# One-bank PSUM tiles in the gate, a stage of its own for the Newton steps, and k turned on TensorE

## The chip, the cores and the metric

The kernel runs on one core of one Trainium2 chip. The metric is the time of one execution on the device in microseconds (us); where a kernel ran several times, the median is given. One core has no other die to compare with, so an execution counts as disturbed (slow) when it is more than 1.5% above the fastest of the same kernel. Ratios are the mean time of one kernel's fast runs over the mean of the other's fast runs of the same rounds, so they are not quite the ratio of the medians quoted beside them.

The engines are called as in the profile: PE is TensorE's matrix multiplication, PEld its weight loading, ACT ScalarE, DVE VectorE, POOL GpSimd (which issues the loads), SP SyncE (which issues the transposes and the stores).

## The reference, cut to what matters

```python
# 8 batches, 8 heads, 576 positions, head size 64; m = 32 landmarks
q_lm, k_lm = means of q and of k over blocks of 18 positions
A  = softmax(q @ k_lm.T / 8); Bm = softmax(q_lm @ k_lm.T / 8); C = softmax(q_lm @ k.T / 8)
Z  = Bm.T / (norm1(Bm) * norminf(Bm) + 1e-6)
for _ in range(6): Z = 2 * Z - Z @ Bm @ Z          # Newton steps
x  = A @ Z @ C @ v                                 # heads side by side: 576 x 512
x1, x2, x3 = split(x @ w_proj, 3)                  # 512 -> 3 * 512
conv = irfft(rfft(x2, axis=1) * rfft(filter), n=576)
out  = (x1 * conv * x3) @ w_out
```

## The kernel before

For each batch there are three pieces of work. `front` makes landmarks, Bm and the start of Newton; `back` makes the six Newton steps, the two sets of scores, C v, and the normalised A with its transpose AT; `gate` makes the projection, the Fourier transform by matrix multiplication, the product with the filter, the inverse transform and the two factors x1 and x3. `project` is the output projection of the batch before, put in small steps into the gate. A batch's `back` and the next one's `front` are woven ahead of the gate of the batch before. The framework's scheduler decides the final order of the instructions on each engine.

The eight PSUM banks (512 fp32 columns each) were divided so:

```python
ps_w = tile_pool(name="ps_w", bufs=2, PSUM)   # gate, filter, projection: 2 tiles of 2 banks
ps_f = tile_pool(name="ps_f", bufs=2, PSUM)   # front
ps_k = tile_pool(name="ps_k", bufs=2, PSUM)   # back
def wtile(): return ps_w.tile([P, 2, 512], F32, tag="w", name="w")
```

The gate fills a tile of two banks and one instruction empties both:

```python
def g_part(jb):
    pg = wtile()
    for g in range(2):
        for pp in range(2):
            mm(pg[64*pp:64*pp+64, g, :], ZC[...], wproj[...], start=True, stop=True)
    nc.scalar.copy(G[:, :, Dm*jb:Dm*(jb+1)], pg)             # 1024 columns
...
for part in (0, 2):                                          # the factors x1 and x3
    px = wtile()
    for g in range(2):
        for e in range(2):
            mm(px[:, e, 0:HS], G[...], AT[:, g, HS*e:HS*e+HS], start=(g==0), stop=(g==1))
    if part == 0: x1 = ...; nc.scalar.copy(x1, px[:, :, 0:HS])   # 576 columns
    else: nc.vector.tensor_tensor(gt[:, ji], px[:, :, 0:HS], x1, op=ALU.mult)
```

Both q and k, which lie with positions on the partitions, are turned by DMA, one transpose after the other on one queue, for each batch:

```python
nc.sync.dma_start_transpose(kT, kn)     # in front(b)
nc.sync.dma_start_transpose(qT, qn)
```

The softmax here doesn't subtract the row's maximum and nothing guards it: scores larger than these inputs give would overflow.

## Time and profile before

| of the kernel before | |
|---|---|
| time, median of 3 runs | 278.95 us (275.12 to 279.15) |
| span of the profiled run | 277.0 us |
| PE, DVE, ACT, POOL busy | 81, 66, 57, 15% |
| y (the gated product) of batch 1, 5, 6, 7 ends at | 115.44, 219.11, 244.81, 266.84 us |

The end of y is a good milestone: it is the last thing a gate makes, and the gates follow each other strictly. The prediction below shows the page, the stretches and the last gate. Three rows of the page's groups show what the wide tiles cost. A row gives line, engine, operation, what is made from what, shapes and count; then busy us and mean ns of one; then the idle us of that engine just before them and what ended most of it.

```profile
L541 PE MATMUL w<-AT,G 128*128 128x288 f16 x256 | 40.3, 285 | 6.1 <-ACT G L472 3.0
L548 DVE TENSOR_TENSOR gt<-w,x 128x576 bf16<-128x576 f32 x32 | 24.1, 756 | 15.4 <-PE w L541 7.2
L472 ACT CAST G<-w 128x1024 bf16<-128x1024 f32 x24 | 23.6, 1015 | 5.9 <-PE w L468 5.7
```

The factor matmuls wait 6.1 us, 3.0 of them for G and 2.4 for the emptying of gt's tile, and gt on DVE waits for those matmuls in turn.

### The profile page before, as it was taken

The numbers are of one execution on the slowest core, as the hardware profiler recorded it, in microseconds if no ns is written. First come the engines' busy times: TensorE is split into PE (matmuls) and PEld (weight loads), VectorE is DVE, ScalarE is ACT, GpSimd is POOL, SyncE is SP. The second block draws the span as 40 slices with busy tenths as digits, with TensorE's granted clock in tenths as the row PEclk, the third lists the DMA queues.
The fourth block names the chain that finished last, engine by engine and source line by source line (L and its number), as shares of the span: only waits on it lengthen the run. The fifth ranks groups of instructions, "written<-read, shape, count | busy, mean of one in ns | idle before, by whom it ended". The sixth has DMA issues, their size and how long they took to land.

```text
span 277.0 us, 5760 instructions
## 1 busy us (share of the span) xinstructions
PE 224.3 (81%) x2300; PEld 147.0 (53%) x2300; DVE 183.4 (66%) x429; ACT 158.1 (57%) x269; POOL 40.7 (15%) x91
## 2 busy tenths in 40 slices
PE   0315199798989999999999999899978996896870
PEld 0204065465767557756766676587546743543530
DVE  1492215648878795896799679957985596537531
ACT  1156043259658577839855885598467746465430
POOL 8961220141050410211210001000000000000000
PEclk9999999999999999999999999999999999999998
DMA  6999999999999999999999976900140023005006
GB/s 83 189 150 215 205 197 187 152 211 161 183 153 165 169 130 184 216 177 181 219 179 81 225 156 94 231 22 2 37 116 20 4 76 95 2 25 147 2 0 170
DMA packets 70283, 36.10 MB, mean 130 GB/s; under 512 B 51632, under 2 KB 65456, under 8 KB 70256
## 3 DMA queue, kind: packets, MB, share of 16 engines
q0 software_dynamic: 26480, 16.85, 47.2%
q1 hardware_dynamic: 43776, 18.88, 39.1%
q8 instruction: 18, 0.29, 0.5%
q14 instruction: 9, 0.07, 0.1%
HBM read 33.69 MB, written 9.44 MB: 156 GB/s over the span
## 4 chain that ended last, share of the span: by engine, by line
PE 56%; ACT 13%; DVE 13%; DMA 7%; POOL 4%; issue 4%; DVEq 0%; SPq 0%; POOLq 0%
PE w L589 9%; PE w L541 7%; DMA filt<-in_moe_filter_fft_dram 7%; PE w L478 5%; PE pc L327 5%; PE w L556 4%; DVE gt L548 4%; PE w L468 4%; PE pv L351 4%; PE w L498 3%; ACT G L472 3%; ACT EO L560 2%; PE w L433 2%; PE w L558 2%; ACT X L501 2%
## 5 line engine op out<-in xcount | busy, mean ns | idle before, releaser
L541 PE MATMUL w<-AT,G 128*128 128x288 f16 x256 | 40.3, 285 | 6.1 <-ACT G L472 3.0
L548 DVE TENSOR_TENSOR gt<-w,x 128x576 bf16<-128x576 f32 x32 | 24.1, 756 | 15.4 <-PE w L541 7.2
L589 PE MATMUL w<-wout,y 128*128 128x512 bf16 x128 | 31.9, 378 | 1.6 <-DVE y L565 1.1
L541 PEld LDWEIGHTS <-G 128*128 128x128 bf16 x256 | 23.2, 97 | 17.7 <-ACT G L472 6.4
L560 ACT CAST EO<-w 128x576 bf16<-128x576 f32 x32 | 20.4, 638 | 14.0 <-PE w L558 13.7
L472 ACT CAST G<-w 128x1024 bf16<-128x1024 f32 x24 | 23.6, 1015 | 5.9 <-PE w L468 5.7
L556 PE MATMUL w<-IV,Y 128*128 128x288 f16 x128 | 24.7, 285 | 1.6 <-DVE gt L548 1.5
L546 ACT CAST x<-w 128x576 bf16<-128x576 f32 x32 | 20.6, 645 | 7.3 <-PE w L541 6.4
L501 ACT CAST X<-w 128x1024 bf16<-128x1024 f32 x16 | 16.2, 1014 | 14.7 <-PE w L498 14.7
L318 ACT CAST RZ<-pn 128x256 f16<-128x256 f32 x40 | 15.2, 380 | 13.5 <-PE pn L314 10.0
L503 DVE TENSOR_TENSOR T<-X,HH 128x2048 bf16<-128x2048 bf16 x16 | 19.4, 1215 | 4.4 <-ACT X L501 4.2
L319 DVE TENSOR_TENSOR RZ<-RZ,pn 128x64 f16<-128x64 f16 x48 | 10.3, 215 | 15.6 <-ACT RZ L318 12.0
L314 PE MATMUL pn<-RZ 128*128 128x160 f16 (+1 forms) x96 | 15.3, 236 | 5.7 <-DVE RZ L298 3.3
L81 POOL DMA_DIRECT2D qn<-in_q_dram x16 | 12.4, 782 | 43.1 <-PE ptA L394 16.0
L468 PE MATMUL w<-wproj,ZC 128*64 128x512 bf16 x96 | 16.6, 398 | 2.4 <-ACT X L519 2.1
L478 PE MATMUL w<-F,AE 96*128 96x304 f16 x96 | 18.2, 306 | 0.4 <-ACT G L472 0.2
L558 PE MATMUL w<-IV,Y 128*128 128x288 f16 x64 | 18.3, 286 | 0.0
L589 PEld LDWEIGHTS <-y 128*128 128x128 bf16 x128 | 11.6, 97 | 12.4 <-DVE y L565 1.6
L498 PE MATMUL w<-G,Ah 128*128 128x512 bf16 x64 | 17.0, 378 | 0.0
L563 DVE TENSOR_TENSOR sd<-EO 128x576 bf16<-128x576 bf16 x16 | 7.3, 458 | 14.6 <-ACT EO L560 14.6
L351 PE MATMUL pv<-vb,eC 96*128 96x320 bf16 x96 | 16.7, 320 | 0.1
L376 DVE TENSOR_REDUCE rA<-eA 96x48 f32<-96x1536 bf16 x8 | 13.9, 1743 | 3.7 <-ACT eA L330 3.7
(139 smaller groups left out, 450.6 us busy)
## 6 DMA issues: line engine op xcount, KB each, us to landing
kn<-in_k_dram POOLq DMA_DIRECT2D x8, 576.0 KB, 14.4
qn<-in_q_dram POOLq DMA_DIRECT2D x16, 288.0 KB, 10.4
vb<-in_v_dram POOLq DMA_DIRECT2D x16, 288.0 KB, 12.0
out_dram<-os SPq DMA_DIRECT2D x24, 192.0 KB, 2.7
out_dram<-os SPq DMA_DIRECT2D x16, 128.0 KB, 2.9
wproj<-in_moe_w_proj_dram POOLq DMA_DIRECT2D x1, 1536.0 KB, 16.8
out_dram<-os SPq DMA_DIRECT2D x24, 64.0 KB, 2.6
out_dram<-o SPq DMA_DIRECT2D x16, 64.0 KB, 2.1
```

The lines of the kernel that those rows point to most:

```text
L351: mm(pv[:, 0:320], eC[:, c, 128 * g:128 * g + 128], vn[:, g, :, c, :], start=(c == 0), stop=(c == NC - 1))
L468: mm(pg[64 * pp:64 * pp + 64, g, :], ZC[:, 2 * g + pp, :, :].rearrange("p h l -> p (h l)"), wproj[:, 2 * g + pp, Dm * jb:Dm * (jb + 1)], s ...
L472: nc.scalar.copy(G[:, :, Dm * jb:Dm * (jb + 1)], pg)
L478: mm(pf[:, par, 0:TW], AE[:, par, c, 128 * g:128 * g + 128], F[:, c, par, :], start=(c == 0), stop=(c == 2))
L498: mm(px[:, t, :], Ah[:, g, par, 128 * t:128 * t + 128], G[:, g, Dm:2 * Dm], start=(g == 0), stop=(g == 1))
L501: nc.scalar.copy(X, px)
L541: mm(px[:, e, 0:HS], G[:, g, lo:lo + P], AT[:, g, HS * e:HS * e + HS], start=(g == 0), stop=(g == 1))
L548: nc.vector.tensor_tensor(gt[:, ji], px[:, :, 0:HS], x1, op=ALU.mult)
L556: mm(pi[:, ji, 0:HS], Y[:, par, t, P * j:P * j + P], IV[:, par, t, :], start=(t == 0), stop=False)
L558: mm(pi[:, ji, 0:HS], Y2[:, P * ji:P * ji + P], IV2[:, jp, par, :], start=False, stop=True)
L560: nc.scalar.copy(EO[:, par], pi[:, :, 0:HS])
L589: mm(po[:, u, :], yv[:, j, P * (2 * ip + u):P * (2 * ip + u + 1)], wout[:, j, :], start=(j == 0), stop=(j == 3))
```

## The change

The intent: (1) the four banks of `ps_w` become four tiles of one bank, and all evacuations of the gate become halves; (2) Newton becomes a stage `inverse` between `front` and `back`, with a PSUM bank of its own (taken from `front`), so four batches are in flight; (3) k is turned by 24 transposes of 96 columns on PE, woven between the Newton steps, instead of by DMA; (4) all output copies `os` go to ACT, where VectorE had half of them. The core of the diff:

```diff
-    ps_w = tile_pool(name="ps_w", bufs=2)          -    ps_f = tile_pool(name="ps_f", bufs=2)
+    ps_w = tile_pool(name="ps_w", bufs=4)          +    ps_f = tile_pool(name="ps_f", bufs=1)
+    ps_i = tile_pool(name="ps_i", bufs=1)
     def wtile():
-        return ps_w.tile([P, 2, 512], F32, tag="w", name="w")
+        return ps_w.tile([P, 512], F32, tag="w", name="w")
 ...
-        nc.sync.dma_start_transpose(kT, kn)        # q's transpose moves from front to inverse
+        def turn(i):                               # in inverse(b), after Newton steps 0, 2, 4
+            pt = ktile("pt", BF16)
+            for u in range(8):
+                mm(pt[:, u*R:(u+1)*R], kn[... 8*i+u ...], ident[:R, :R], is_transpose=True, ...)
+            (nc.scalar.copy if i == 1 else nc.vector.tensor_copy)(kT[... chunk i ...], pt[:, 0:8*R])
 ...
         def g_part(jb):
-            pg = wtile()
             for g in range(2):
+                pg = wtile()
                 for pp in range(2): mm(...)
-            nc.scalar.copy(G[:, :, Dm*jb:Dm*(jb+1)], pg)
+                nc.scalar.copy(G[:, g, Dm*jb:Dm*(jb+1)], pg)
 ...  (the same for the forward and inverse transform, X, and the filter)
-    px[:, e, 0:288] of x1 and x3: 4 matmuls of 288 columns, one copy of 576
+    px of x1 and x3: 2 matmuls of 512 columns, one copy of 512;
+    factors_rest(): the last 64 columns of all 8 in one tile, 16 matmuls of 64 columns
 ...
-            (nc.vector.tensor_copy if ip else nc.scalar.copy)(os, po)      # 1024 columns
+            nc.scalar.copy(os, po)                                         # 512 columns
 ...
-        weave(steps(back, b + 1, NK), steps(front, b + 2, NF), ...)
+        weave(steps(back, b + 1, 12), ...)
         gate(b, pending)
+        weave(steps(inverse, b + 2, 10), steps(front, b + 3, 7))
```

## The prediction

> **What bounds the kernel now.** I read the page first (busy shares, slices, chain), then a table of stretches, then the timeline of the last gate, where nothing else runs.
>
> ```profile
> PE 224.3 (81%) x2300; PEld 147.0 (53%) x2300; DVE 183.4 (66%) x429; ACT 158.1 (57%) x269; POOL 40.7 (15%) x91
> ...
> PE   0315199798989999999999999899978996896870
> ...
> DMA  6999999999999999999999976900140023005006
> ```
>
> Each digit is a fortieth of the span, 6.9 us. There are three stages. Up to slice 5 (33 us) PE is nearly idle and the DMA full. From slice 6 to 31 PE shows 7 to 9. In the last eight slices (222 us on) it falls again. The stretches, cut at the recurring output projections, say the same:
>
> ```profile
> core 0: us, PE busy (x) PEld busy (x) DVE busy (x) ACT busy (x) POOL busy (x), PEclk, DMA share, GB/s
> 144.70:170.40 25.70, 25.12 (x277) 17.05 (x275) 20.31 (x49) 18.29 (x32) 1.02 (x2) 1.00 1.02 140
> ...
> 222.00:245.00 23.00, 18.74 (x146) 10.71 (x145) 16.39 (x31) 12.63 (x17) 0.00 (x0) 1.00 0.19 52
> 245.00:277.00 32.00, 20.08 (x137) 10.58 (x135) 13.35 (x20) 12.04 (x16) 0.00 (x0) 0.97 0.27 75
> ```
>
> The middle is a steady 25.7 us per batch, PE busy in 25.1 of them. But that counts pipelined ends. The spacing of starts is the real need: a run of n matmuls lasts (n-1) spacings plus one duration, so 8 of the projection in 1.89 us at 378 ns each give 216 ns; the factor matmuls of 288 columns (4 in 0.65 us, 285 ns each) 122 ns; the transposes ptA (12 in 0.68, 215 each) 42 ns. Summing such spacings over one batch of the middle I get 23.1 us: gate 3.9 (factors) + 2.9 (inverse transform) + 1.7 (X) + 1.6 (forward transform) + 1.6 (G) + 0.5, projection 3.9, scores 2.2, pv 1.6, and about 3.2 for front, Newton and transposes. So about 2.6 us of each 25.7 is waiting, part of it the weight loads of narrow tiles. PE bounds the middle; there is little to win there.
>
> The last gate:
>
> ```profile
> 254.80 0.66 PE L541 MATMUL w<-AT,G 128*128 128x288 f16 x4 [0.67 <-ACT G L472]
> 255.71 1.19 PE L541 MATMUL w<-AT,G 128*128 128x288 f16 x8 [0.25 <-ACT G L472]
> 256.49 0.76 DVE L548 TENSOR_TENSOR gt<-w,x 128x576 bf16<-128x576 f32 x1 [1.81 <-PE w L541]
> 257.30 0.65 PE L541 MATMUL w<-AT,G 128*128 128x288 f16 x4 [0.40 <-DVE gt L548]
> ...
> 258.06 0.76 DVE L548 TENSOR_TENSOR gt<-w,x 128x576 bf16<-128x576 f32 x1 [0.81 <-PE w L541]
> ```
>
> Here is a ping-pong over two buffers: PE fills one, VectorE or ScalarE empties it, PE may go on. All three engines show idle time in brackets. From y of batch 6 (244.8) to y of batch 7 (266.85) it takes 22.05 us for about 14 us of PE spacings.
>
> **What the Trainium skill says.** (1) "PSUM — Partial Sum Buffer", The four PSUM rules: one matmul output is at most one bank, 512 fp32 columns. A wide tile here is two banks, so two tiles are the same four banks as four single ones; the trace agrees in that no matmul exceeds 512 columns. (2) "TensorE: Matmul & The Clock Gate", Back-to-back issue gap: N/2.4 + 2.5 ns when warm, thus 215.8 and 122.5 ns for 512 and 288 columns; the trace has 216 and 122. (3) "VectorE: DVE Perf Modes", The TRN2 errata: ScalarE reading PSUM costs 172 cycles plus one per column at 1.2 GHz[...], so halved tiles pay it twice; that is 997 and 570 ns for 1024 and 512 columns, and the trace has 1015 and 589. (4) "DMA: Bandwidth & Descriptors", Issuing engines are not separate DMA queues: all DMAs share 16 engines. The trace agrees: k transposes take 13.3 us in the median beside loads, but 5.7 us (160.57 to 166.28) where the loads have ended.
>
> **The change part by part.**
>
> *k transposes to PE.* Eight DMA transposes go. 24 PE transposes of 96 columns per batch come: 24 x 42 ns = 1.0 us of PE, in the stage where PE is the bound. Their evacuation is one ScalarE copy of 768 columns, by row G's scaling 640 + 162 = 0.80 us, and two VectorE copies; AT's 576 two-byte columns take 447 ns, so 768 take about 550, 1.1 us together. The relieved DMA matters only before 33 us: the filter lands at 32.7 us and the chain shows 7% of the span for it. The k transpose of batch 0 (7.9 to 13.1 us) mostly precedes the start of that queue's big loads (11.8), so only about 2 us of the 5 come back: -2 us.
>
> *512-column factors.* 32 x 122 = 3.90 us becomes 16 x 215 + 16 x 28 (a 64-column remainder, spaced like pk and pz at 25) = 3.9 us. Nothing for PE.
>
> *Single-bank evacuation.* Consecutive ScalarE copies start a little before the former ends (two G in 1.93 us: 0.91 apart; 512 columns by exp: 0.49). Per batch: G 2.7 to 2.9, Ah 1.1 to 1.2, X 1.8 to 2.0, x1 2.1 to 2.2, EO 2.1 to 2.4, os 0.9 to 2.0 (VectorE's os of 1.2 us moves here), k 0.7. ScalarE goes from 18.1 to about 20.6 us, VectorE stays at 20 (-1.1 os, +0.9 k, +0.1 rest). Both stay below PE.
>
> *Middle, sum.* PE need 23.1 + 1.0 = 24.1. With today's 2.6 us of waiting the batch would be 26.7; finer buffers should take perhaps a third of it, since of some 15 us by which start spacings exceed their usual value between 93 and 196 us (four batches) 4.1 stand before the factors. I choose 26.3: +0.6 over some six batches, +3.5 us.
>
> *Newton as its own stage.* It takes the six-step chain (pn, ScalarE copy, VectorE add) off the way from scores to pv, but in the middle that chain already lies beside the gate; worth nothing there. The last two gates have no Newton left over them, so batch 7's is done earlier.
>
> *Last gate.* From y of 6: PE now has projection 3.44 + X 1.72 + narrow X 0.45 + G 1.1 + rest of projection 0.5 = 7.2 us; with four buffers PE runs ahead of ScalarE (13 copies of 0.49, 6.4 us), so about 7.5 where 9.9 stood (244.9 to 254.8): -2.4. Factors and inverse: PE 6.8, VectorE 5.2 (four gt of 0.61, one of 0.33, four sd, two y), ScalarE 4.6: PE-bound, plus 0.4 in front and 2.4 for the last EO, sd, sd, y behind: 9.6 where 12.05 stood, -2.4. The end: the first output copy ends after 4 instead of 8 matmuls and takes 0.59 instead of 1.01 us, and the ten stores that follow are issued one by one on SP at some 0.5 us each: -0.9. Together -5.7.
>
> *Gates 5 and 6* (196 to 245 us) have the same ping-pong with less work beside them, PE need 21.3 of 26 and 16.7 of 23 us. I give them -1.5 and -2.5.
>
> Sum: -2 + 3.5 - 5.7 - 4 = -8.2 us of 278.95: 270.7, put as **270.5 us**.
>
> **The rivals.** *A: PE pays for it.* The middle is PE-bound and gets 1.0 us more of PE per batch; moreover the front now has one PSUM bank instead of two, so pq must wait until ScalarE has emptied pk (Pk 388 ns plus its queue), and ScalarE stands in line with 2.5 us more work. For it: PE's 9s. Against it: in the built order transposes of k stand between pk and pq as filling. If each batch loses 1.5 us over today, the middle costs +9 and the sum is -3: 276. *B: ScalarE becomes the bound.* 20.6 of some 26 us is 79%, yet in strict order; if os copies wait for PE while X waits behind them, PE stalls in the projection, where 4 os now stand between X copies. That makes 278 to 282. *C: the waits were the true price.* If single banks remove most of the 2.6 us, the batch is 25 us and the kernel 262 to 264. For it: the waits before the factors name G's and gt's evacuation. *D: the DMA was holding the start more than I think* (slices 1 to 20 at 9). Then up to 5 us rather than 2 go there; but PE waits of 34 to 93 us name VectorE's Bn, Cv, A and AT, not loads.
>
> **Range and chances.** A and C are the wide ones, each about a fifth, B a tenth. 80% range 263 to 279. Two per cent is 5.6 us, thus 273.4 and 284.5: faster 0.65, same 0.31, slower 0.04.
>
> **What would show it.** Filter landing near 31 us and first G matmul near 54 (today 56.1); projections in the middle 26.3 us apart with ScalarE busy near 21; k transposes spaced near 42 ns; from y of 6 to y of 7 17 us instead of 22; no DMA transposes of k, and DMA idle digits earlier than slice 25. Wrong would be: a middle period above 27.5 (A or B, told apart by what PE waits for, pk's evacuation or the wide tiles) or below 25.3 (C), or a last gate still above 20 us.

## More of the kernel before

The waits of PE from y of batch 1 to y of batch 5 are small and many (us in total, times, longest):

```profile
PE w L599 <- ACT X L501: 0.7, 1, 0.7
PE w L468 <- ACT X L519: 0.7, 1, 0.7
PE w L541 <- ACT G L472: 0.6, 3, 0.2
PE w L541 <- DVE gt L548: 0.6, 2, 0.4
```

These are four of nine rows. In each a matmul into a w tile waits until ACT or DVE has emptied a w tile; for the third the reason can also be the data, since the factors read the G that this copy makes.

## The result, and the profile after

The changed kernel took 258.39 us (257.89 to 261.96, four runs) where the kernel before took 279.05 us in the same rounds: ratio 0.930, 95% interval 0.917 to 0.942. Its profiled run was the disturbed one, so the same kernel was run again later (five rounds, label after2): 258.21 us against 278.4 us, again 0.930 (0.922 to 0.937). The profile of that second visit is the one read here. The change gained about 20 us, where 8 had been predicted, and the time lies below the predicted range.

From the page of the changed kernel:

```profile
span 256.9 us, 6283 instructions
...
PE 219.9 (86%) x2492; PEld 142.7 (56%) x2492; DVE 185.8 (72%) x446; ACT 188.0 (73%) x401; POOL 40.5 (16%) x91
...
PE   0732099699689999999999999899999999999990
...
DMA  5999999979999996999389944891015002403305
```

From slice 12 on PE shows 8 or 9 up to the last slice but one, where before the last eight slices went down to 6, 6 and 7. ACT did 158.1 us of work before and does 188.0 now: all output copies are its own (18.4 us for 8.1), it has eight copies of k (6.4 us), and halved tiles pay the fixed cost of an evacuation twice (1015 ns for 1024 columns of G before, 604 ns for 512 now). The loads last nearly as long as before (the DMA digits fall at slice 28, 173 us, where they fell at slice 27, 180 us).

The stretches from y to y (us from and to, length, then busy us and count of PE, PEld, DVE, ACT and POOL, granted clock, DMA share, GB/s):

```profile
129.06:155.11 26.05, 25.79 (x305) 16.78 (x303) 21.09 (x52) 21.44 (x49) 3.04 (x5) 1.00 1.01 137
207.80:231.10 23.30, 23.11 (x221) 14.32 (x219) 17.60 (x37) 19.70 (x46) 0.00 (x0) 1.00 0.20 52
231.10:256.90 25.80, 18.83 (x137) 9.50 (x135) 11.16 (x20) 15.07 (x33) 0.00 (x0) 0.93 0.34 92
```

These answer to the three stretches shown in the prediction, cut at y now and not at projections. A batch of the middle takes about the same time as before. The last whole batch (the second row) is shorter and PE is idle in only 0.2 us of it; the last stretch is 25.8 us.

The last gate:

```profile
238.71 1.96 PE L561 MATMUL w<-AT,G 128*128 128x512 f16 x8
...
240.35 1.29 DVE L566 TENSOR_TENSOR gt<-w,x 128x512 bf16<-128x512 f32 x2 [1.63 <-PE w L561]
...
240.51 0.63 PE L575 MATMUL w<-AT,G 128*128 128x64 f16 x16
...
240.98 0.41 PE L588 MATMUL w<-IV,Y 128*128 128x288 f16 x2
...
241.55 1.50 ACT L592 CAST EO<-w 128x288 bf16<-128x288 f32 x4
...
242.45 1.89 PE L561 MATMUL w<-AT,G 128*128 128x512 f16 x8
```

No PE row has brackets: eight factor matmuls run in one stretch while ACT and DVE follow behind. Where before PE stood still after each tile or two, it now runs ahead of its readers. From y of batch 6 to y of batch 7 it takes 16.82 us, where 22.03 us stood.

PE's waits in the middle, from y of batch 1 to y of batch 5, are these two and no more:

```profile
PE pk L218 <- DMA kn<-in_k_dram: 1.0, 1, 1.0
PE pn L325 <- DVE cm L288: 0.2, 1, 0.2
```

The w tiles have gone from the list. Where the 20.1 us between the two profiled spans went, by these milestones:

| stretch | before, us | after, us | difference | predicted |
|---|---|---|---|---|
| start to y of batch 1 | 115.44 | 103.07 | -12.4 | -2 |
| y of 1 to y of 4 | 77.47 | 79.21 | +1.7 | +3.5 over some six batches |
| y of 4 to y of 6 | 51.90 | 48.82 | -3.1 | -4 |
| y of 6 to y of 7 | 22.03 | 16.82 | -5.2 | -4.8 |
| y of 7 to the end | 10.19 | 8.99 | -1.2 | -0.9 |

Everything but the first row is about as predicted. The start gave over ten us more than it was given: -7.8 us up to y of batch 0 (80.56 for 88.31 us), and -4.6 from there to y of batch 1 (22.51 for 27.13 us).

### The profile page after: what moved, and what is told of

Read it like the earlier page. It is cut to its first block, busy times and chain, and to the rows that moved or that the text cites. A ratio compares the mean times of both kernels' runs of the same rounds, so it can differ in the third digit from the quotient of the medians.

```text
span 260.3 us, 6267 instructions
## 1 busy us (share of the span) xinstructions
PE 220.4 (85%) x2476; PEld 143.1 (55%) x2492; DVE 185.3 (71%) x446; ACT 187.9 (72%) x401; POOL 40.8 (16%) x91
## 2 busy tenths in 40 slices
DMA packets 51597, 31.40 MB, mean 121 GB/s; under 512 B 32944, under 2 KB 46768, under 8 KB 51568
## 4 chain that ended last, share of the span: by engine, by line
PE 52%; DMA 22%; issue 11%; POOL 6%; ACT 5%; DVE 3%; POOLq 0%
DMA kn<-in_k_dram 14%; PE w L629 9%; PE w L561 9%; DMA qn<-in_q_dram 7%; PE w L588 4%; PE w L517 4%; PE pv L371 4%; PE pc L351 4%; PE w L486 3%; PE w L496 3%; ACT EO L592 2%; PE w L590 2%; PE pt L314 2%; PE pn L325 1%; PE w L532 1%
## 5 line engine op out<-in xcount | busy, mean ns | idle before, releaser
L561 PE MATMUL w<-AT,G 128*128 128x512 f16 x128 | 32.1, 380 | 0.3
L631 ACT COPY os<-w 128x512 f32<-128x512 f32 x32 | 18.4, 587 | 16.7 <-PE w L629 16.4
L490 ACT CAST G<-w 128x512 bf16<-128x512 f32 x48 | 25.7, 603 | 5.4 <-PE w L486 5.3
L592 ACT CAST EO<-w 128x288 bf16<-128x288 f32 x64 | 24.1, 399 | 1.9 <-PE w L590 1.8
L566 DVE TENSOR_TENSOR gt<-w,x 128x512 bf16<-128x512 f32 x32 | 21.9, 686 | 4.2 <-ACT x L564 2.2
L86 POOL DMA_DIRECT2D qn<-in_q_dram x16 | 12.4, 778 | 73.1 <-PE w L496 17.6
L564 ACT CAST x<-w 128x512 bf16<-128x512 f32 x32 | 19.1, 600 | 5.6 <-PE w L561 4.6
L314 PE MATMUL pt<-ident,kn 96*128 96x96 bf16 x192 | 14.2, 217 | 7.5 <-DMA kn<-in_k_dram 7.5
L519 ACT CAST X<-w 128x512 bf16<-128x512 f32 x32 | 17.8, 593 | 1.2 <-PE w L517 1.2
L486 PE MATMUL w<-wproj,ZC 128*64 128x512 bf16 x96 | 18.6, 401 | 0.0
L561 PEld LDWEIGHTS <-G 128*128 128x128 bf16 x128 | 11.6, 97 | 12.3 <-ACT G L490 2.5
L330 DVE TENSOR_TENSOR RZ<-RZ,pn 128x64 f16<-128x64 f16 x48 | 10.3, 215 | 8.3 <-ACT RZ L329 7.5
```

The source lines that it names most:

```text
L486: mm(pg[64 * pp:64 * pp + 64, :], ZC[:, 2 * g + pp, :, :].rearrange("p h l -> p (h l)"), wproj[:, 2 * g + pp, Dm * jb:Dm * (jb + 1)], star ...
L490: nc.scalar.copy(G[:, g, Dm * jb:Dm * (jb + 1)], pg)
L561: mm(px, G[:, g, lo:lo + P], AT[:, g, 0:512], start=(g == 0), stop=(g == 1))
L566: nc.vector.tensor_tensor(gt[:, j, 0:512], px, x1, op=ALU.mult)
L592: nc.scalar.copy(EO[:, par, j % 2], pi[:, 0:HS])
```

## The experiments

The first theory was that the single-bank tiles made nearly all of the gain, at the start too, and that k on PE is a cost. Its rivals were: that the start is a matter of the clock (the record of the granted clock shows full speed from 60.1 us on in the kernel before, but already from 38.1 us on in the changed one, with a lapse from 48.3 to 51.7, and half-speed matmuls before that); that k's transposes, gone from the DMA, free the start; and that the new stage does it. Where an expectation gives a theory a letter, its own words say what it stands for. All runs gave correct results.

### The parts alone, on the kernel before

**e3_gate**: the kernel before with the changed gate, filter and projection only (four one-bank tiles); k by DMA, no stage of its own for Newton.

```diff
-    ps_w = tile_pool(name="ps_w", bufs=2); wtile: [P, 2, 512]
+    ps_w = tile_pool(name="ps_w", bufs=4); wtile: [P, 512]
+    gate, filter_tables, project as in the changed kernel
```

> The kernel before with only the gate, filter and projection in single-bank tiles. Theory W (waits at the wide tiles were the price in the middle): the middle falls by about 1 to 1.5 us per batch and the last gate from 22 to about 17 us, so 262 to 268 us. Rival S (the own stage for Newton does it): the middle keeps 26 us per batch, only gates 5 to 7 gain, 268 to 273 us.

255.38 us against 277.68 us, ratio 0.921 (0.912 to 0.929). One part alone does more than the whole change. It was run again beside the changed kernel:

> The single-bank gate alone once more, on the same chip as after2: 254 to 256 us if its first result holds, with batches 24.7 us apart.

255.36 us, ratio 0.915 (0.905 to 0.925), where the changed kernel had 258.21 us and 0.930 in the same rounds; the intervals overlap slightly, so the difference of 1% is likely and not certain. In the first profile of it y of batch 1 ends at 106.84 us (-8.6 against before), the four batches of the middle take 99.0 us (-4.7), the next one -3.1, the last gate -5.2, the end -1.2: together -22.8 us. Of the start's 8.6 us, 4.6 lie between y of batch 0 and y of batch 1 (22.55 us, where 27.13 stood). That stretch, first before and then here:

```profile
88.30:115.40 27.10, 26.00 (x293) 17.95 (x292) 21.34 (x52) 19.33 (x35) 3.94 (x6) 1.00 1.36 172
```

```profile
84.30:106.80 22.50, 22.32 (x254) 14.38 (x255) 18.97 (x47) 18.48 (x43) 4.44 (x6) 1.00 1.42 155
```

It is not the same work: PE ran 293 matmuls before and runs 254 now, because fewer scores and Newton steps of later batches fall into it. So the 4.6 us are in part waits that went and in part work that moved to later stretches (from y of 5 to y of 6 it is 197 matmuls, where it was 170). A batch of the middle from the second profile, the same columns as above, and all of PE's waits between 106 and 205 us in it:

```profile
131.08:155.54 24.46, 24.38 (x279) 15.34 (x276) 19.84 (x50) 20.97 (x48) 2.41 (x4) 1.00 1.31 149
```

```profile
PE pc L327 <- ACT eA L330: 0.2, 1, 0.2
```

**e2_kpe**: the kernel before with k turned on PE in `front`, all else as it was.

```diff
-        nc.sync.dma_start_transpose(kT, kn)
+        turn(0); ...; turn(1); ...; turn(2)      # between the parts of front
```

> The kernel before with only k turned on PE (in the front stage, in three parts). Theory C: DMA relief is worth 2 us at the start at most, PE has 1.0 us more per batch; 277 to 285 us unless the clock happens to be granted earlier, which the clock record shows. Theory D: 5 us or more at the start, 270 to 275 us, with the clock still half until about 60 us.

287.77 us, ratio 1.037 (1.028 to 1.046): it costs 10 us. A middle batch takes 27.07 us where 25.92 stood (+1.15), and y of batch 1 comes at 120.43 us, 5 us late. So freeing the DMA of k's transposes is no gain by itself.

**e4_stage**: the kernel before with the stage alone (wide tiles, k by DMA).

```diff
-    ps_f = tile_pool(name="ps_f", bufs=2)
+    ps_f = tile_pool(name="ps_f", bufs=1); ps_i = tile_pool(name="ps_i", bufs=1)
+    def inverse(b): ...                          # Newton, both DMA transposes
```

> The kernel before with the stage of its own for Newton alone (k and q turned by DMA in that stage, front PSUM down to one bank, Newton in its own bank). Theory W: within 2% of the kernel before. Rival S: 268 to 273 us.

269.73 us against 275.67 us, ratio 0.978 (0.968 to 0.988): a gain of some 6 us, though at 2% the verdict is unclear. Its profiled run was a slow one: one middle batch took 29.87 us, the two after it 24.97 and 24.98.

**e8_nostage**: e3_gate and e2_kpe together, no stage.

> The kernel before with single-bank gate and k on PE, Newton left among the scores. If the parts add: 255.4 + 10 = 263 to 267 us. If the stage of its own is what makes room for k on PE, it is above the changed kernel's 258 by 5 us or more; if the stage is worth nothing, 256 to 260 us.

269.1 us, ratio 0.980 (0.973 to 0.987), unclear at 2%. Against e3_gate, k on PE without the stage costs some 14 us (6% by the ratios); a middle batch takes 26.33 us, +1.58 over e3_gate's.

### The parts taken back from the changed kernel

**e6_kdma**: the changed kernel with k turned by DMA again.

```diff
+        nc.sync.dma_start_transpose(kT, kn)      # in inverse, ahead of q's
-                turn(it // 2)
```

> The changed kernel with k turned by DMA again, all else kept. If k on PE costs its 24 spacings of 42 ns per batch, as it did alone in the kernel before (+10 us there): 248 to 253 us. If the DMA relief at the start is worth as much (first G matmul at 46.5 us in the changed kernel against 54.9 with the gate alone): 256 to 261 us.

258.09 us, ratio 0.936 (0.928 to 0.945): the same as the changed kernel. But it comes by the same time in another way. A middle batch takes 24.86 us (1.32 less), and y of batch 0 ends at 89.13 us instead of 80.56. PE's waits between 40 and 90 us begin so:

```profile
PE pc L343 <- DMA qT<-qn: 4.6, 1, 4.6
PE pc L343 <- DMA kT<-kn: 2.0, 1, 2.0
```

With Newton in a stage ahead, the first G matmul comes early (47.3 us, as in the changed kernel), and PE then stands waiting for transposes that queue behind each other. In the changed kernel only q is in that queue: its transposes for batches 1 to 3 end at 52.7, 63.2 and 78.5 us, where here they end at 56.8, 78.7 and 87.3 us. So beside the stage k on PE saves 7 to 9 us at the start and gives them back, 1.3 us in each later batch.

**e7_wide**: the changed kernel with the two wide tiles and the old gate.

> The changed kernel with gate, filter and projection put back into two-bank tiles, stage and k on PE kept. Theory W (the single banks carry the whole gain): it is no faster than the kernel before, 276 to 288 us, and the last gate takes 22 us again. Rival S (the stage carries part of it): 268 to 274 us.

286.04 us, ratio 1.040 (1.033 to 1.047). The single banks are worth 28 us here, but some 13 us of it is an accident of one batch. Of the waits of all engines between 76 and 102 us:

```profile
POOL qn L86 <- DMA qT<-qn: 15.0, 1, 15.0
...
PE pk L218 <- DMA kn<-in_k_dram: 13.1, 1, 13.1
```

A load of q on POOL's queue waited 15 us for the transpose that still read its buffer, the load of k behind it waited too, and PE waited 13.1 us for k. The middle batches beyond it take 26.06 us, against 26.18 in the changed kernel: beside the stage and k on PE, single banks are worth nothing in the middle. They are worth 5.2 us in the last gate (22.04 against 16.82), where Newton and the scores of later batches no longer lie between the tiles. And its y of batch 0, before the accident, ends at 79.30 us, where the kernel before has 88.31 and the changed kernel 80.56. So up to there the changed kernel's gain needs no single banks: the stage and k on PE make it together.

The eight medians together. They come from several calls, whose kernel before had 275.7 to 279.1 us, so differences below 3 us say little:

| us | wide tiles | single banks |
|---|---|---|
| no stage, k by DMA | 277.7 (before) | 255.4 |
| no stage, k on PE | 287.8 | 269.1 |
| stage, k by DMA | 269.7 | 258.1 |
| stage, k on PE | 286.0 (with the accident) | 258.2 (the change) |

The single banks gain in every row. "Single banks" is here the whole changed gate: four tiles, half-size evacuations, factors of 512 columns and output copies on ACT; of these only the output copies were taken back by themselves (g5_osdve). With k by DMA the stage gains beside wide tiles (-8 in the table), not beside single banks (+3). The likely reason is that both remove the same waits. With k on PE it gains beside single banks too (-11). A middle batch with k by DMA takes 25.92 us with neither, 24.75 with single banks, 24.97 with the stage (the batches after the disturbed one), 24.86 with both.

### Is it the clock at the start?

**e1_warm** adds 24 matmuls of 512 columns, whose results nobody reads, to the kernel before, in front of the filter's matmuls, so that the clock is up when these come; landmarks of batch 1 get a lower priority. **e1_ctl** has the change of priority alone.

```diff
+        with tc.high_priority(offset=-400) if b == 1 else nullcontext():   # pk, pq of batch 1
 ...
+            if b == 0 and cc == 2:                                         # e1_warm only
+                pd = wtile()
+                with tc.high_priority(), tc.issue_after(last.ins):
+                    for i in range(24): mm(pd[:, i % 2, :], F[...], F[...], start=True, stop=True)
```

> The kernel before, with 24 matmuls of 512 columns that nobody reads put on PE between the third scores of batch 0 (26 us) and the filter's matmuls (33.7 us), and pk and pq of batch 1 put behind the filter's matmuls. Theory C (clock): in the kernel before PE ran at half its clock until 60 us, and the gain of the changed kernel before its first gate comes from a clock that was granted at 35 us. Then the clock is full by 33 us here, the filter's matmuls start 215 ns apart instead of 426, the first G matmul comes near 49 us instead of 56, and the time is 6 to 9 us below that of the control e1_ctl. Theory D (loads): the gain comes from fewer DMA transposes beside the loads. Then the first G matmul stays within 2 us of 56 and the time within 3 us of the control, since 24 idle-time matmuls change no load.

> The same order of pk and pq of batch 1 as in e1_warm without the 24 matmuls. Both theories: within 1.5% of the kernel before, clock still half until some 50 to 60 us.

277.78 us (0.996, 0.985 to 1.008) and 275.0 us (0.993, 0.986 to 1.001) against 277.68 us. The filter's matmuls, first without and then with the added ones:

```profile
33.71 1.87 PE L436 MATMUL w<-fs,F 96*128 96x512 f16 x4 [7.43 <-DVE fs L427]
```

```profile
35.83 0.81 PE L443 MATMUL w<-fs,F 96*128 96x512 f16 x3
```

The clock did come up: four in 1.87 us, some 426 ns apart, became three in 0.81 us, some 215 ns apart. Yet the first G matmul came at 56.49 us, where the kernel before has 56.05 and the control 52.29, and the time is 2.8 us above the control's, where the clock theory had 6 to 9 us below. The time won was spent in other waits of PE (33 to 57 us of e1_warm):

```profile
PE pq L231 <- DMA qn<-in_q_dram: 4.1, 2, 2.5
PE pk L222 <- DMA kn<-in_k_dram: 2.4, 1, 2.4
```

With these waits the clock fell back to half from 46.4 to 60.0 us, so the test covers the filter's stretch and not all of the start. The control did not do what was expected of it either: its clock was not half until 50 us but full from 37.6 to 47.8 and again from 54.6 us. It has y of batch 1 at 111.65 us, 3.8 us before the kernel before, and from there to the end both take 161.6 us. So an early clock, or the priority alone, goes with 3.8 us at the start; which of the two it is, this pair does not tell.

Two profiles of one kernel are a cleaner test. e3_gate shows full clock only from 57.5 us on, hardly earlier than the kernel before; e3_again, the same kernel, from 41.2 us on with lapses. Their first G matmuls come at 54.87 and 51.57 us, and their y of batch 1 at 106.84 and 105.93 us: the early clock went with 0.9 us. So an early clock is not needed for the gain, and did not bring it where it was forced. But up to some 4 us of the 12.4 at the start may be a matter of the single profile of the kernel before, whose fast runs took 273.5 to 279.6 us in all.

### What of the single banks does it?

The changed gate has smaller evacuations, four tiles instead of two, and a bank that comes back by itself. Two kernels were meant to take these apart, two more ask for other bounds, all from e3_gate and beside a kernel before of 274.18 us.

**g2_bufs2** has half the memory, two one-bank tiles.

```diff
-    ps_w = tile_pool(name="ps_w", bufs=4)
+    ps_w = tile_pool(name="ps_w", bufs=2)
```

> e3_gate with two single-bank buffers instead of four. Theory R: PE can be only one piece ahead, slower than the kernel before, 285 us or more, last gate above 22 us. Rival E: 255 to 265 us.

281.77 us, ratio 1.029 (1.017 to 1.042): slower than before, though at 2% the verdict is unclear. The last gate takes 23.59 us. Theory R's 285 us were not reached; rival E is out.

**g4_pair** has the same four banks and the same half-size evacuations as e3_gate, but hands the banks out as halves of a two-bank tile, which only comes free when both halves are read.

```diff
-        return ps_w.tile([P, 512], F32, tag="w", name="w")
+        if not pair:
+            t = ps_w.tile([P, 2, 512], F32, tag="w", name="w")      # bufs=2
+            pair.extend([t[:, 1], t[:, 0]])
+        return pair.pop()
```

> The gate alone in single-bank pieces (e3_gate), but the pieces come as the two halves of one two-bank tile, so that a half is filled and emptied by itself while PE gets the memory back only when both halves have been read. Theory R (it is the return of buffers one bank at a time): most of the gain goes, 268 to 280 us, last gate above 20 us. Rival E (it is the smaller evacuations, which end sooner and start after half the matmuls): 254 to 260 us, last gate near 17 us.

294.14 us, ratio 1.072 (1.064 to 1.081): nearly 40 us above e3_gate, and outside what either theory gave. A middle batch takes 27.34 us and the last gate 25.91. From the timeline of its last gate, one row of DVE and three of PE:

```profile
269.03 0.69 DVE L551 TENSOR_TENSOR gt<-w,x 128x512 bf16<-128x512 f32 x1 [1.85 <-PE w L546]
269.77 0.59 PE L546 MATMUL w<-AT,G 128*128 128x512 f16 x2 [0.21 <-DVE gt L551]
271.04 0.40 PE L573 MATMUL w<-IV,Y 128*128 128x288 f16 x2 [0.67 <-ACT x L549]
...
271.76 0.63 PE L560 MATMUL w<-AT,G 128*128 128x64 f16 x16 [0.20 <-DVE gt L551]
```

The kernel does not do what its expectation says. The second row fills the second half of the tile whose first half the first row reads, and it begins only when that read is over (269.72 us); the fourth row waits in the same way. Only the third waits for a new tile. A build of this kernel shows it throughout: for all 150 wide tiles the semaphores let PE fill the later half only after the earlier one has been read. So a tile never had more than one half under way, and g4_pair, with four banks, had no more than two pieces under way at a time, like g2_bufs2. It is no test of banks that come back in pairs; that stays untested.

Taken together, the two still answer something. Both have the smaller evacuations and both are slower than the kernel before, so smaller evacuations alone are not it (rival E). Four banks alone are not it either, since g4_pair has them. What e3_gate has and neither of them has is four pieces under way at once, each freed by itself: 255.4 us with four, 281.8 and 294.1 with two.

**g5_osdve** moves every second output copy from ACT to DVE, to see whether ACT bounds e3_gate.

```diff
-            nc.scalar.copy(os, po)
+            (nc.vector.tensor_copy if (i0 // P) % 2 else nc.scalar.copy)(os, po)
```

> e3_gate with two of the four output copies of a batch on VectorE, as in the kernel before. If ScalarE (21 of 24.7 us per batch) stands in the way, 250 to 254 us; if PE bounds the middle, within 1% of e3_gate.

262.17 us, ratio 0.947 (0.935 to 0.959), slower than e3_gate's 0.921 though ACT has less to do (170.4 us of busy time for 176.9); neither expectation came true. DVE has more to do (185.5 for 175.5 us), so the test moves two things at once. It shows that relief of ACT gains nothing here. That ACT does not bound the middle is seen in the row of e3_again above: PE is busy in 24.38 of 24.46 us.

**g7_bufs5** asks whether a fifth tile would gain more: no stage, k by DMA, five one-bank tiles, the fifth taken from `front`, which is left with one.

> e3_gate with five single-bank buffers for the gate and one bank less for the front stage. If waits for gate buffers are still there: 250 to 254 us. If four are enough: within 1% of e3_gate, or slower by the front's lost bank.

260.19 us, ratio 0.939 (0.927 to 0.951; the profiled run was a slow one). A middle batch takes 24.56 us and the last gate 16.80, against 24.75 and 16.81 with four: hardly any use there. The start has y of batch 0 at 90.31 us, where e3_gate has 84.29. That the bank is missed in `front` is likely and not shown, for this slow profile also has half the clock up to 65.9 us.

### A version that takes both

If k on PE pays at the start and costs later, it should be used at the start alone. **h1_first3** is the changed kernel with k on PE in the first three batches and by DMA in the others, **h2_first2** the same with two.

```diff
+        if b >= 3:                                # h2_first2: 2
+            nc.sync.dma_start_transpose(kT, kn)
 ...
-                turn(it // 2)
+                if b < 3:
+                    turn(it // 2)
```

> The changed kernel once more. If stage and k on PE take back more than they give: 1% or more above e3_again (258 against 255). If the difference was one of calls: within 0.5% of it.

> The changed kernel with k turned on PE for batches 0 to 2 and by DMA from batch 3 on, when the loads have less in hand. If k on PE saves at the start and costs 1.15 us per later batch: second y near 103 us, later batches 24.9 instead of 26.0 us apart, so 250 to 253 us. If both effects are not so separate: 256 us or more.

> The same for batches 0 and 1 only: 250 to 254 us if the third batch's transpose no longer meets the rush of loads, 254 to 258 if it does.

Against 278.4 us before and 258.21 us of the changed kernel, h1_first3 takes 251.55 us (0.907, 0.897 to 0.917) and h2_first2 253.17 us (0.911, 0.904 to 0.917). A middle batch of h1_first3:

```profile
127.14:151.98 24.84, 24.80 (x284) 15.70 (x283) 19.87 (x49) 21.14 (x49) 2.66 (x4) 1.00 1.18 179
```

It has the early start of the changed kernel (y of batch 0 at 80.11 us) and the middle of e6_kdma (24.85 us a batch, where the changed kernel has 26.18). It is 2.6% faster than the changed kernel by the medians, and the fastest of all that were run; it is 1.5% below e3_again, where the intervals overlap (0.897 to 0.917 and 0.905 to 0.925). Whether two or three batches are better stays open: the intervals overlap.

## Why the prediction was right or wrong

**Right: the last gate and the end.** -2.4 and -2.4 were given for the last gate and -0.9 for the end; -5.2 and -1.2 were measured. The reading behind it, that four tiles let PE run ahead of its readers, is what the timeline shows; with two such tiles (g2_bufs2) the last gate takes 23.59 us. Gates 5 and 6, given -4 together, gave -3.1.

**Nearly right: the price of k on PE.** 24 x 42 ns = 1.0 us per batch was given; the pairs of kernels with and without it show 1.15, 1.32 and 1.58 us. The trace has eight of these transposes in 0.50 us at 206 ns each, (0.50 - 0.206) / 7 = 42 ns apart, as assumed; the rest is what comes with them.

**Right as a sum, not in its parts: the middle.** 26.3 us a batch were predicted and 26.18 measured. "finer buffers should take perhaps a third of it", about 0.9 of 2.6 us of waiting, was rather low: single banks alone took 1.2 us (25.92 to 24.75). And "worth nothing there", said of the Newton stage, is wrong with wide tiles, where the stage took 0.95 us (25.92 to 24.97, in undisturbed batches of a slow run), and right with single banks, which leave it nothing to take.

**Wrong: the start.** The failed step is "so only about 2 us of the 5 come back: -2 us", which was all that the whole stretch up to y of batch 1 was given. It measured -12.4, and this term alone makes 10.4 of the 12 us by which the time was missed. The step looked at the DMA's loads only. Two things stood in its place.

First, up to y of batch 0 (-7.8 us), the stage and k on PE together, by a path that the prediction did not see. e7_wide, which has these two and wide tiles, has y of batch 0 at 79.30 us, where 88.31 stood. The stage brings the first G matmul from 56.1 to about 47 us (46.00 in e4_stage, 46.59 in e7_wide), and this is only kept when q's transposes no longer queue with k's. With single banks, each of the two without the other loses it: e6_kdma waits 6.6 us for transposes and has y of batch 0 at 89.13 us; e8_nostage has its first G at 57.38 us and y of batch 0 at 88.70. With wide tiles k on PE alone has 89.05 us (e2_kpe) and the stage alone 85.42 (e4_stage, a slow run), within the 3.4 us by which e1_ctl, with none of the parts, came earlier too (84.89).

Second, from y of batch 0 to y of batch 1 (-4.6 us), the single banks: 22.5 us in e3_gate and the changed kernel alike, at least 26.8 in every kernel with wide tiles. The gates there were given no gain. How much of it is waits that went, and how much work that moved to later stretches, was not taken apart.

The prediction asked whether the relieved DMA would let the filter land earlier; it did land 1.9 us earlier (30.83 for 32.71 us), as foreseen, and that was the small part.

**The rivals.** C ("the waits were the true price", 262 to 264 us) came nearest, and its cause is the right one, but its place was not the middle: with k on PE the batch there stayed at 26.2 us. A did not come: k's added 1.3 us are offset by the waits that went. B did not come either: the time is far below its 278, and relief of ACT (g5_osdve) gained nothing. D put up to 5 us at the start by way of the DMA. Relief of the DMA alone is not it, since e2_kpe has the same relief and is slower; it counts only together with the stage, as queueing of transposes.

**The signs that it named.** The filter landing (31 predicted, 30.83), the period (26.3 and 26.18), ACT's busy time per batch (near 21, 21.44; the parts that the prediction lists sum to 20.8, not to its 20.6), the spacing of k's transposes and the last gate (17 and 16.8 us) came as said. The first G matmul was to be near 54 us and came at 47.75: this sign showed the failed step at once. The DMA's idle digits were to begin before slice 25 and begin at slice 28: the transposes' 4.7 MB are gone (36.10 to 31.40 MB), but the loads wait mostly for PE to have read their buffers, not for the DMA.

What stays open: how much of the start's 12.4 us is the early clock or the one profile of the kernel before (up to some 4 us, see e1_ctl); why k on PE costs the start 5 us in e2_kpe, beyond its share of PE time; whether two banks that are filled independently and come back together would do; and what part of e7_wide's 28 us is the accident, which is known from its trace alone.

## What to carry to other kernels

When an engine waits for buffers to be emptied, ask how many pieces it can have under way at once before asking for more memory: here four banks with four pieces under way gave 255 us, the same banks and evacuations with two pieces under way 294 us, and a fifth tile, taken from another stage, gave nothing more. Check in the trace that a test kernel really does what it was built for: the halves of one tile were filled one after the other. Halving the evacuations cost ScalarE some 9 us of busy time (176.9 for 158.1 us in e3_gate, of which 10.3 us are the output copies from VectorE) and was still worth it. Two remedies for the same wait do not add up, so test each alone before paying for both; one part of this change was as good as the whole. And a remedy that pays in one stage and costs in the others, as k on PE does, can be kept to the batches in which it pays.

## What the Trainium skill lacked or had wrong

- "PSUM — Partial Sum Buffer": it tells what a bank is and how to guard it, but puts no number on how many tiles PE needs under way. With one-bank tiles and the same evacuations two took 281.8 us, four 255.4 us and five, the fifth taken from another stage, 260.2 us.
- "TensorE: Matmul & The Clock Gate", Back-to-back issue gap: it states a sustained 131 ns per matmul of 512 columns in streams of weight loads and matmuls, and calls the 216 ns of its formula the isolated case. Here such a stream, eight output projections in 1.89 us at 378 ns each, is (1.89 - 0.378) / 7 = 216 ns apart.
- The same page, Part 4: PE-mode transpose: it gives durations (some 275 to 390 ns) but no spacing. Here transposes of 96 columns last 206 ns and are 42 ns apart, and the spacing decides what they cost. The gap formula of the point above, which the page gives for matmuls, makes 42.5 ns of 96 columns, so it holds for these transposes too.
- The same page, Part 1: The HAM clock gate: it has full clock after one busy window of about 3.4 us. Here PE counts as busy in 20.43 of the 22.30 us from 33.7 to 56.0 us of the kernel before, yet the record shows full clock only from 60.06 us; with 24 dense matmuls of 512 columns ahead (e1_warm) it shows it from 32.73 us, and in their control without them (e1_ctl) from 37.55 us. What counts as busy is not told by the busy share of a profile, and no run here settles it.
- "DMA: Bandwidth & Descriptors", Latency and other measured facts: it has 261 GB/s for a DMA transpose, measured on one kernel. Here 96 x 1536 two-byte elements (295 KB) took 5.7 us from issue to landing where the loads had ended, which is 52 GB/s, and 13.3 us in the median of all eight.
